# Linear attention beside a routed expert on one core: the layer norm by Ln and Exp on ScalarE, fewer and larger first loads, and a rewritten order of the head

## The chip, the cores and the metric

The kernel runs on one core of a Trainium2 chip. The metric is device time in microseconds (us) of one execution; lower is better. Times shown are the median of several runs, and one further execution was taken with the hardware profiler. TensorE is called PE here, VectorE DVE, ScalarE ACT, GpSimd POOL, and SyncE, which issues most of the DMAs, SP. PEld is PE's weight load, which runs beside its matmuls.

## The reference

```
x = A_x                                   # 1 x 2048 x 640, bf16
xn = layernorm(x)                         # (x - mean) / sqrt(var + 1e-5), no gain, no bias
out = x + A(xn, A_wqkv, A_wo) + B(xn, B_w_r, B_w_gate, B_w_up, B_w_down)

A: q, k, v = xn @ wqkv, 32 heads of 20 columns each
   phi(t) = where(t > 0, t + 1, exp(t)) + 1e-6
   kv = sum over s of phi(k)^T v ;  z = sum over s of phi(k)
   o  = phi(q) kv / (phi(q) z + 1e-6) ;  result o @ wo
B: r = xn @ w_r ;  the 8 rows of largest r go through
   y = (silu(xs @ w_gate) * (xs @ w_up)) @ w_down, times sigmoid(r)
   result: xn, with y added in these 8 rows
```

## The kernel before

The 2048 rows are 16 tiles of 128 rows. Everything is in SBUF: `XX[:, t, 1, :]` is the raw x of tile t, `XX[:, t, 0, :]` its normalised form, `xnT` the transposed normalised rows (5 blocks of 128 columns), `wk` the k part of `wqkv`, `pk` phi(k). The whole kernel is one hand-written order of instructions: the program text is the order in which each engine gets its work, each engine takes its own in that order, and waits are added where data ask for them. An engine whose next instruction waits does nothing else meanwhile.

The head is the part before the loop `for t in range(4, T)`. For tiles 0 to 3 it goes step by step through what the loop does for the others:

- **Norm.** `ln_a(t)` and `ln_b(t)` take statistics of the two halves of 320 columns on DVE, `ln_g(t)` joins them to mean and variance (`MV`). `ln_s(t)` adds epsilon on DVE and takes the square root as a power of 0.5 on POOL. `ln_c(t)` makes mean - x (on DVE in the head, on ACT in the loop), and `ln_xn(t)` takes the reciprocal of the root and multiplies, both on DVE. Tiles 1 and 5 get their statistics from ACT instead (`ln_act`, `ln_msq`, `ln_var`).
- **Transposition.** Tiles 0 to 3 are transposed by PE (`tr_pe`: 3 blocks into one PSUM bank, 2 into the next, each then copied to `xnT` by ACT); the others by a DMA that SP issues (`tr_dma`).
- **K(t)**: xn of tile t times `wk` in two halves of 320 columns, 5 matmuls each. The second half has one column more, which is `w_r`, so that r comes out of the same matmuls; `w_r` is loaded as 5 rows, turned by PE and copied by ACT into that column. The halves of `wk` are two blocks in one tile, of row pitch 320 and 321 elements.
- **PHe, PHr, PHb**: exp and relu of K's halves on ACT, and their combination to `pk` on DVE.
- **G(t)**: the products of xn^T and phi(k), 9 matmuls that add up in PSUM banks 0 to 5 over all tiles. `rcopy1` takes tile 1's r out of bank 5. `ones(t)` sets one column of xn to 1 by POOL before G.

In the loop one tile does K(t), PHb(t-1), `ln_xn(t+2)`, `tr_dma(t+2)`, PHe and PHr, the statistics of tiles t+3 and t+4, and G(t-1).

Behind the loop come q (by blocks of 512 rows), the products with `wv` and `wo` that make `Mb`, the routed rows, and the output; the change touches there only the row pitch of `Mb`, which shares its space with `wk`.

The first loads on SP, in order: x of tiles 0, 1 and 2; the first half of `wk`; x of tile 3; five loads for the second half of `wk` (one for each block of 128 rows); x of tiles 4-5, 6-7, 8-11 and 12-15; and a DMA transposition of zeros into a part of `xnT` that is written again later. While these run, PE multiplies zeros (`warm4`, `warm`), which the kernel sets in SBUF by DVE first. `bm2` is a mask; POOL makes 32 rows of it and three DMAs copy them to the other rows.

Of the kernel before, what the change touches and what calls it, by code (L numbers as in the profile page):

```python
# [38 lines left out]
def kernel(  # L39
# [78 lines left out]
    zero32 = zero[:].bitcast(F32)  # L118

    def warm4(n):  # L120
        for _ in range(n):
            pe.matmul(PS[:, 7, :], lhsT=zero32[:, 0:P],  # L122
                      rhs=zero32[:, 0:256].unsqueeze(1).to_broadcast([P, 2, 256]), start=True, stop=True)

    def warm(n, w=512):
        for _ in range(n):
            pe.matmul(PS[:, 7, 0:w], lhsT=zero[:, 0:P], rhs=zero[:, 0:w], start=True, stop=True)
# [29 lines left out]
    def ln_a(t):  # L157
        sts[t] = tmp.tile([P, 2, nc.vector.BN_STATS_DIM], F32, tag="stats", name="stats", bufs=3)
        dve.bn_stats(out=sts[t][:, 0, :], in_=XX[:, t, 1, 0:320])  # L159
# [787 lines left out]
```

## Time and profile before

| | |
|---|---|
| median of 3 runs | 108.91 us (108.5 to 109.03) |
| the profiled execution | 108.45 us |
| its span, first to last instruction | 106.7 us |
| PE busy | 101.7 us, 95% of the span |
| DVE, ACT, POOL busy | 84.3, 74.8 and 27.8 us |
| loop's first matmul, K(4) | 17.78 us after the span's start |

How to read the rows: in a timeline the first number is the start in us from the span's start, the second the time until the last of the merged instructions ended, then engine, line, operation, output<-inputs, shapes, and xN for N merged instructions; brackets give idle time of the engine before it and what ended it. A queue of DMAs has a q behind its engine (SPq). A wait row has the total, the number of times and the longest wait. A row of a stretch (A:B) has the length, then for PE, PEld, DVE, ACT and POOL the busy time with the number of instructions, then the granted PE clock, the DMA engines' mean busy share and GB/s. A row of a group of instructions has the busy time and the mean ns of one behind the first bar. A row of a DMA has the size of one transfer and the median time from issue to landing in us.

### The profile page before, as it was taken

The numbers are of one execution on the slowest core, as the hardware profiler recorded it, in microseconds if no ns is written. First come the engines' busy times: TensorE is split into PE (matmuls) and PEld (weight loads), VectorE is DVE, ScalarE is ACT, GpSimd is POOL, SyncE is SP. The second block draws the span as 40 slices with busy tenths as digits, with TensorE's granted clock in tenths as the row PEclk, the third lists the DMA queues.
The fourth block names the chain that finished last, engine by engine and source line by source line (L and its number), as shares of the span: only waits on it lengthen the run. The fifth ranks groups of instructions, "written<-read, shape, count | busy, mean of one in ns | idle before, by whom it ended". The sixth has DMA issues, their size and how long they took to land.

```text
span 106.7 us, 2600 instructions
## 1 busy us (share of the span) xinstructions
PE 101.7 (95%) x923; PEld 62.6 (59%) x923; DVE 84.3 (79%) x207; ACT 74.8 (70%) x163; POOL 27.8 (26%) x79
## 2 busy tenths in 40 slices
PE   5979999999999999999999999999999999999990
PEld 1245656666666666667556545655656677777760
DVE  1789997999998999974898996729598696888870
ACT  4649996888877777888497999997688499200000
POOL 7437235456222222000000593500006200000410
PEclk9999999999999999999999999999999999999999
DMA  2999961435566875889998999901560224796344
GB/s 75 272 276 336 339 82 38 81 74 77 112 141 135 118 138 123 175 219 381 234 399 274 352 339 386 311 26 31 170 237 0 63 95 126 177 364 227 123 126 123
DMA packets 23247, 19.68 MB, mean 184 GB/s; under 512 B 10818, under 2 KB 21698, under 8 KB 23234
## 3 DMA queue, kind: packets, MB, share of 16 engines
q1 hardware_dynamic: 22712, 19.45, 65.5%
q8 instruction: 7, 0.11, 0.4%
q0 software_dynamic: 288, 0.01, 0.4%
q10 hardware_dynamic: 234, 0.06, 0.2%
q14 instruction: 6, 0.05, 0.2%
HBM read 13.80 MB, written 3.65 MB: 164 GB/s over the span
## 4 chain that ended last, share of the span: by engine, by line
PE 84%; DVE 7%; POOL 2%; issue 2%; ACT 1%; DVEq 0%; POOLq 0%
PE PS L502 21%; PE PS L755 19%; PE PS L251 15%; PE PS L291 15%; PE PS L296 3%; PE PS L122 2%; PE PS L678 2%; PE PS L715 2%; DVE XX L213 1%; DVE pk L286 1%; POOL s L199 1%; DVE stats L162 1%; PE PS L566 1%; PE PS L737 1%; PE PS L310 1%
## 5 line engine op out<-in xcount | busy, mean ns | idle before, releaser
L251 PE MATMUL PS<-wk,xnT 128*128 128x320 bf16 (+1 forms) x160 | 24.7, 300 | 0.6 <-ACT xnT L224 0.4
L291 PE MATMUL PS<-pk,XX 128*128 128x512 bf16 x80 | 23.2, 378 | 0.1
L502 PE MATMUL PS<-xnT,wq 128*128 128x512 bf16 x100 | 23.0, 380 | 0.0
L755 PE MATMUL PS<-Mb,pqT 128*128 128x320 bf16 (+2 forms) x165 | 22.1, 295 | 0.0
L251 PEld LDWEIGHTS <-xnT 128*128 128x128 bf16 x160 | 15.4, 98 | 7.4 <-ACT xnT L224 0.9
L755 PEld LDWEIGHTS <-pqT 128*128 128x128 bf16 x165 | 15.8, 97 | 6.4 <-issue 0.2
L267 ACT ACTIVATE ek<-PS 128x320 bf16<-128x320 f32 x32 | 14.3, 446 | 5.2 <-PE PS L251 5.2
L502 PEld LDWEIGHTS <-wq 128*128 128x128 bf16 x100 | 11.3, 118 | 9.0
L557 DVE SCALAR_TENSOR_TENSOR pqT<-qe,qr 128x512 bf16<-128x512 bf16 x20 | 13.5, 683 | 2.0 <-ACT qr L509 1.7
L768 DVE TENSOR_TENSOR o<-PS,XX 128x640 bf16<-128x640 f32 x15 | 12.2, 820 | 3.6 <-PE PS L755 2.8
L508 ACT ACTIVATE qe<-PS 128x512 bf16<-128x512 f32 x20 | 12.2, 609 | 3.8 <-PE PS L502 3.3
L270 ACT ACTIVATE rk<-PS 128x320 bf16<-128x320 f32 x32 | 14.4, 449 | 0.0
L199 POOL TENSOR_TENSOR s<-t,halfc 128x1 bf16<-128x1 bf16 x14 | 8.6, 617 | 21.7 <-DVE t L198 21.7
L296 PE MATMUL PS<-pk,XX 128*128 128x128 bf16 x64 | 14.0, 219 | 0.0
L286 DVE SCALAR_TENSOR_TENSOR pk<-ek,rk 128x640 bf16<-128x640 bf16 x16 | 13.0, 815 | 0.9 <-ACT rk L270 0.7
L291 PEld LDWEIGHTS <-XX 128*128 128x128 bf16 x80 | 7.7, 98 | 8.1
L509 ACT ACTIVATE qr<-PS 128x512 bf16<-128x512 f32 x20 | 12.1, 607 | 0.0
L204 ACT ACTIVATE c<-XX,MVf 128x640 bf16<-128x640 bf16 x10 | 8.4, 839 | 1.7 <-DVE MVf L165 1.6
L241 ACT ACTIVATE XX<-XX,MR,SR 128x640 bf16<-128x640 bf16 x11 | 9.4, 914 | 0.0
L159 DVE BATCH_NORM_STATS2 stats<-XX 128x6 f32<-128x320 bf16 x14 | 6.8, 486 | 1.9 <-DMA XX<-in_A_x_dram 1.9
L213 DVE TENSOR_SCALAR XX<-c,SR 128x640 bf16<-128x640 bf16 (+2 forms) x17 | 6.3, 377 | 1.3
L296 PEld LDWEIGHTS <-XX 128*128 128x128 bf16 x64 | 6.2, 97 | 1.3 <-issue 0.4
(125 smaller groups left out, 104.7 us busy)
## 6 DMA issues: line engine op xcount, KB each, us to landing
out_dram<-o SPq DMA_DIRECT2D x15, 160.0 KB, 2.3
wg<-in_B_w_gate_dram SPq DMA_DIRECT2D x5, 384.0 KB, 8.3
wu<-in_B_w_up_dram SPq DMA_DIRECT2D x5, 384.0 KB, 5.9
wd<-in_B_w_down_dram SPq DMA_DIRECT2D x1, 1920.0 KB, 10.7
XX<-in_A_x_dram SPq DMA_DIRECT2D x2, 640.0 KB, 7.1
wv<-in_A_wqkv_dram SPq DMA_DIRECT2D x5, 160.0 KB, 2.9
wq<-in_A_wqkv_dram SPq DMA_DIRECT2D x1, 800.0 KB, 5.4
hi_d<-XX SPq DMA_DIRECT2D x1, 800.0 KB, 4.5
```

The costliest lines, as they stand in the source:

```text
L251: pe.matmul(PS[:, b + h, off(t, h) : off(t, h) + w], lhsT=xnT[:, kc, t * P : (t + 1) * P], rhs=wkh[h][:, kc, 0:w], start=(kc == 0), stop=( ...
L267: act.activation(phis[t][0][:, h * HW : (h + 1) * HW], phi_src(t, h, b), AF.Exp)
L270: act.activation(phis[t][1][:, h * HW : (h + 1) * HW], phi_src(t, h, b), AF.Relu)
L286: dve.scalar_tensor_tensor(out=pk[:, t, :], in0=ek[:], scalar=1.0, in1=rk[:], op0=ALU.min, op1=ALU.add)
L291: pe.matmul(PS[:, a, :], lhsT=lhsT, rhs=pk[:, t, 0:512], start=(t == 0), stop=(t == T - 1),)
L296: pe.matmul(PS[:, 5, a * P : (a + 1) * P], lhsT=lhsT, rhs=pk[:, t, 512:D], start=(t == 0 and a == 0), stop=(t == T - 1), skip_group_check= ...
L502: pe.matmul(PS[:, bank, :], lhsT=by5(wq[:, kc, :])[:, m, :], rhs=xnT[:, kc, tb * TBLK : (tb + 1) * TBLK], start=(kc == 0), stop=(kc == KC ...
L508: act.activation(e, PS[:, bank, :], AF.Exp)
L509: act.activation(r, PS[:, bank, :], AF.Relu)
L557: dve.scalar_tensor_tensor(out=pqT[:, m, tb * TBLK : (tb + 1) * TBLK], in0=e, scalar=1.0, in1=r, op0=ALU.min, op1=ALU.add,)
L755: pe.matmul(PS[:, b_, 0 : c1 - c0], lhsT=pqT[:, kc, t * P : (t + 1) * P], rhs=Mb[:, kc, c0:c1], start=(kc == 0), stop=(kc == KC - 1))
L768: dve.tensor_tensor(out=ot[:].rearrange("p (h c) -> p h c", h=2), in0=PS[:, b : b + 2, 0:HW], in1=XX[:, t, 1, :].rearrange("p (h c) -> p h ...
```

## The change

- The norm becomes one pass: `ln_r(t)` takes Ln of variance + epsilon and then Exp of -0.5 times that, both on ACT with one value a row, which gives 1/sqrt directly; `ln_xn(t)` subtracts the mean and multiplies in one DVE instruction. `ln_s`, `ln_c`, `ln_act` and what belongs to them go, also in the loop. All tiles get their statistics from DVE.
- `wk` has one row pitch of 656 elements: 640 columns, the column of `w_r` at 640, and 15 unused. It comes in two loads of whole rows, 3 blocks and 2.
- Loads on SP, in order: x of tiles 0 and 1, `wk` in two, x of tiles 2-3, 4-7 and 8-11, the transposition of zeros. x of tiles 12-15 is loaded after the transposition of tile 5.
- Tile 3 is transposed by DMA. PE's transposition of tiles 0 to 2 is split in blocks 0-1 and 2-4 (`tr_mm`), with the copies (`tr_cp`) on ACT, or on DVE for the second part of tiles 0 and 2. K of tiles 0 to 2 is split alike: `KA` are its first two matmuls of a half, `KB` the other three.
- The matmuls of zeros take a constant that is there from the program's start, three of them in fp32.
- `bm2`'s rows are copied by POOL, at the start.
- The order of the head is written anew.

```
-    wk = st([P, KC * (D + 1)], BF16, "wk", "wkM")
+    wk = st([P, KC, WS], BF16, "wk", "wkM")
...
-    halfc = st([P, 1], BF16, "halfc")
-    epsb = st([P, 1], BF16, "epsb")
+    eps5 = st([P, 1], F32, "eps5")
+    lnv = st([P, T], F32, "lnv")
-    wkh = [wk[:, 0 : KC * HW].rearrange("p (k c) -> p k c", k=KC),
-           wk[:, KC * HW : KC * (D + 1)].rearrange("p (k c) -> p k c", k=KC)]
...
-    ld(sp, XX[:, 2, 1, :], x_v[:, 2, :])
-    ld(sp, wkh[0], wqkv_v[:, :, D : D + HW])
-    ld(sp, XX[:, 3, 1, :], x_v[:, 3, :])
...
+    for a, b in ((0, 3), (3, KC)):
+        ld(sp, wk[:, a:b, 0:D], wqkv_v[:, a:b, D : 2 * D])
+    for a, b in ((2, 4), (4, 8), (8, 12)):
+        ld(sp, XX[:, a:b, 1, :], x_v[:, a:b, :])
+    sp.dma_start_transpose(xnT[:, 0:4, S - P : S], zero[:])
+
+    def warm4(w):
+        pe.matmul(PS[:, 7, 0:w], lhsT=nc.const_aps.tensor(0.0, (P, P), F32),
+                  rhs=nc.const_aps.tensor(0.0, (P, w), F32), start=True, stop=True)
+
...
-    warm4(1)
+    warm4(512)
+    warm4(256)
     pe.transpose(PS[:, 3, :].bitcast(BF16)[:, 0:KC], wr[:], ident[0:KC, 0:KC])
-    warm4(1)
-    warm(1)
-    act.copy(wkh[1][:, :, HW], PS[:, 3, :].bitcast(BF16)[:, 0:KC])
-    for kc in range(KC):
-        ld(sp, wkh[1][:, kc, 0:HW], wqkv_v[:, kc, D + HW : 2 * D])
+    warm4(512)
+    act.copy(wk[:, :, D], PS[:, 3, :].bitcast(BF16)[:, 0:KC])
...
+    def ln_r(t):
+        act.activation(lnv[:, t : t + 1], MV[:, t, 1:2], AF.Ln, bias=eps5[:])
+        act.activation(SR[:, t : t + 1], lnv[:, t : t + 1], AF.Exp, scale=-0.5)
+
+    def ln_xn(t, parts=((0, D),)):
+        for a, b in parts:
+            dve.tensor_scalar(out=XX[:, t, 0, a:b], in0=XX[:, t, 1, a:b], scalar1=MVf[:, t, 0:1],
+                              scalar2=SR[:, t : t + 1], op0=ALU.subtract, op1=ALU.mult)
+
+    TRP = ((0, 2), (2, KC))
+
+    def tr_mm(t, h, b0):
+        k0, k1 = TRP[h]
+        pt = PS[:, b0 + h, :].bitcast(BF16)
+        for kc in range(k0, k1):
+            pe.transpose(pt[:, (kc - k0) * P : (kc - k0 + 1) * P], XX[:, t, 0, kc * P : (kc + 1) * P], ident[:])
+
+    def tr_cp(t, h, b0, eng):
+        k0, k1 = TRP[h]
+        src = PS[:, b0 + h, :].bitcast(BF16)[:, 0 : (k1 - k0) * P].rearrange("p (k c) -> p k c", c=P)
+        dst = xnT[:, k0:k1, t * P : (t + 1) * P]
         if eng is act:
...
+            act.copy(dst, src)
         else:
...
+            dve.tensor_copy(dst, src)
 
...
-    def K(t, hs=(0, 1), b=6):
+    def K(t, hs=(0, 1), b=6, ks=range(KC)):
...
-                    rhs=wkh[h][:, kc, 0:w],
+                    rhs=wk[:, kc, h * HW : h * HW + w],
...
+    def bm2_copies(gs):
         for g in gs:
+            pool.tensor_copy(bm2[32 * g : 32 * g + 32, :], bm2[0:E2, :])
...
```

The new order of the head, from behind the definitions to the loop:

```
consts_e(); bm2_copies((1, 2, 3)); KA, KB = (range(0, 2), range(2, KC)); ln_a(0); ln_b(0); ln_a(1)
ln_g(0); ln_b(1); ln_r(0); ln_g(1); ln_xn(0, ((0, 2 * P),)); ln_r(1); ln_xn(0, ((2 * P, D),))
tr_mm(0, 0, 0); ln_xn(1); tr_cp(0, 0, 0, act); tr_mm(0, 1, 0); ones(0); tr_mm(1, 0, 2)
tr_cp(0, 1, 0, dve); K(0, (0,), 6, KA); tr_cp(1, 0, 2, act); tr_mm(1, 1, 2); ones(1)
K(0, (0,), 6, KB); ln_a(2); tr_cp(1, 1, 2, act); K(0, (1,), 6, KA); ln_b(2); PHe(0, 0)
K(1, (0,), 4, KA); PHr(0, 0); ln_g(2); K(0, (1,), 6, KB); ln_a(3); ln_r(2); K(1, (1,), 4, KA); ln_b(3)
K(1, (0,), 4, KB); PHe(0, 1); ln_xn(2); PHr(0, 1); ln_g(3); tr_mm(2, 0, 0); PHe(1, 0, 4); PHb(0)
K(1, (1,), 4, KB); tr_cp(2, 0, 0, act); tr_mm(2, 1, 0); ones(2); ln_r(3); K(2, (0, 1), 6, KA)
tr_cp(2, 1, 0, dve); PHr(1, 0, 4); ln_a(4); PHe(1, 1, 4); ln_xn(3); tr_dma(3); ones(3); PHr(1, 1, 4)
K(2, (0, 1), 6, KB); rcopy1(5); ln_b(4); PHe(2, 0); G(0, (0, 1, 4, 2, 3)); PHb(1); PHr(2, 0)
PHe(2, 1); ln_g(4); ln_a(5); ln_r(4); ln_b(5); PHr(2, 1); G(1); ln_xn(4); tr_dma(4); ln_g(5); PHb(2)
ln_r(5); K(3); ln_xn(5); tr_dma(5); ld(sp, XX[:, 12:16, 1, :], x_v[:, 12:16, :]); ln_a(6); PHa(3)
ln_b(6); G(2); ln_g(6); ln_r(6)
```

The loop:

```
     for t in range(4, T):
         K(t)
         ones(t)
         PHb(t - 1)
-        if t + 3 < T and t < 5 and t + 3 not in ACTS:
+        if t + 3 < T and t < 5:
             ln_a(t + 3)
         if t + 2 < T:
             ln_xn(t + 2)
             tr_dma(t + 2)
         PHa(t)
         if t + 3 < T:
-            if t + 3 in ACTS:
-                ln_act2(t + 3)
-                ln_var(t + 3)
-            else:
-                ln_b(t + 3)
-                ln_g(t + 3)
-                ln_s(t + 3)
-            ln_c(t + 3, act)
-        if t + 4 < T and t + 4 in ACTS:
-            ln_act1(t + 4)
-        if t + 4 < T and t >= 5 - 1 and t + 4 not in ACTS:
+            ln_b(t + 3)
+            ln_g(t + 3)
+            ln_r(t + 3)
+        if t + 4 < T and t >= 5 - 1:
             ln_a(t + 4)
...
```

More of the change, by code (lines that the diff above doesn't have):

```diff
@@ L26 @@
 ZD = 4 * P
-ACTS = ()
 TF = 11
+WS = 656
 BF16 = mybir.dt.bfloat16
@@ L390 @@
-    ln_var(1)
+    ln_b(1)
+    ln_r(0)
+    ln_g(1)
+    ln_xn(0, ((0, 2 * P),))
+    ln_r(1)
+    ln_xn(0, ((2 * P, D),))
+    tr_mm(0, 0, 0)
+    ln_xn(1)
+    tr_cp(0, 0, 0, act)
+    tr_mm(0, 1, 0)
+    ones(0)
+    tr_mm(1, 0, 2)
+    tr_cp(0, 1, 0, dve)
+    K(0, (0,), 6, KA)
+    tr_cp(1, 0, 2, act)
+    tr_mm(1, 1, 2)
+    ones(1)
+    K(0, (0,), 6, KB)
     ln_a(2)
-    ln_xn(1)
+    tr_cp(1, 1, 2, act)
+    K(0, (1,), 6, KA)
     ln_b(2)
+    PHe(0, 0)
+    K(1, (0,), 4, KA)
+    PHr(0, 0)
```

182 lines of the change are left out of this document (54 added, 128 removed).

## The prediction

> **What bounds the kernel now.** I read the page first (who is busy), then the waits of PE, then the timelines of PE, DVE, ACT and SP over the first 18 us.
>
> ```profile
> span 106.7 us, 2600 instructions
> PE 101.7 (95%) x923; PEld 62.6 (59%) x923; DVE 84.3 (79%) x207; ACT 74.8 (70%) x163; POOL 27.8 (26%) x79
> PE PS L122 <- DVE MVf L109: 1.2, 1, 1.2
> PE PS L251 <- ACT xnT L224: 0.4, 1, 0.4
> PE PS L220 <- DVE XX L213: 0.2, 1, 0.2
> ```
>
> PE is busy for 95% of the span, and the three waits are all that it has, all at the start. The change leaves the matmuls as they are, except five PE transposes. So its effect is how much earlier or later PE gets past the head. As the mark I take the start of K(4), the first projection of the main loop; behind it PE is a closed row. The timeline of PE up to there:
>
> ```profile
> 5.22 0.38 PE L127 MATMUL PS<-zero 128*128 128x512 bf16 x1
> 5.82 0.48 PE L220 MATMUL PS<-ident,XX 128*128 128x128 bf16 x5 [0.22 <-DVE XX L213]
> 6.73 0.85 PE L251 MATMUL PS<-wk,xnT 128*128 128x320 bf16 x5 [0.43 <-ACT xnT L224]
> 7.70 1.83 PE L251 MATMUL PS<-wk,xnT 128*128 128x321 bf16 x10
> 9.54 0.45 PE L220 MATMUL PS<-ident,XX 128*128 128x128 bf16 x5
> 9.83 2.23 PE L251 MATMUL PS<-wk,xnT 128*128 128x321 bf16 x15
> 11.90 0.45 PE L220 MATMUL PS<-ident,XX 128*128 128x128 bf16 x5
> 12.19 0.38 PE L291 MATMUL PS<-pk,XX 128*128 128x512 bf16 x1
> 13.49 1.53 PE L251 MATMUL PS<-wk,xnT 128*128 128x320 bf16 x10
> 15.18 0.38 PE L291 MATMUL PS<-pk,XX 128*128 128x512 bf16 x1
> 17.78 1.53 PE L251 MATMUL PS<-wk,xnT 128*128 128x320 bf16 x10
> 19.15 0.38 PE L291 MATMUL PS<-pk,XX 128*128 128x512 bf16 x1
> ```
>
> K(4) starts at 17.78, and its 10 matmuls take 19.15 - 17.78 = 1.37 us (0.137 each). G(0) takes 13.49 - 12.19 = 1.30, five transposes 12.19 - 11.90 = 0.29. From the first K at 6.73 the work is 4 K (5.48), 3 G (3.90) and the transposes of tiles 1 to 3 (0.87): 10.25 of the 11.05 us. The missing 0.8 shows: the x10 at 7.70 lasts until 9.54, 0.47 over 1.37; K(3) at 13.49 is through at 14.86, and the next row starts at 15.18, 0.32 later. The change can thus gain 0.8 from these holes, 0.29 from tile 3's transposes, and whatever the first K starts before 6.73.
>
> **The change, part by part.** First the chain of tile 0. DVE and ACT now, and the forms nearest to the new ones:
>
> ```profile
> 3.15 0.50 DVE L159 BATCH_NORM_STATS2 stats<-XX 128x6 f32<-128x320 bf16 x1 [1.92 <-DMA XX<-in_A_x_dram]
> 3.56 0.48 DVE L162 BATCH_NORM_STATS2 stats<-XX 128x6 f32<-128x320 bf16 x1
> 4.07 0.21 DVE L165 BATCH_NORM_AGGREGATE MVf<-stats 128x2 bf16<-128x12 f32 x1
> 4.31 0.16 DVE L198 TENSOR_SCALAR t<-MVf 128x1 bf16<-128x1 bf16 x1
> 5.24 0.16 DVE L211 RECIPROCAL SR<-s 128x1 f32<-128x1 bf16 x1 [0.16 <-POOL s L199]
> 5.44 0.51 DVE L213 TENSOR_SCALAR XX<-c,SR 128x384 bf16<-128x384 bf16 x2
> 5.87 0.48 DVE L159 BATCH_NORM_STATS2 stats<-XX 128x6 f32<-128x320 bf16 x1
> 9.10 0.39 DVE L213 TENSOR_SCALAR XX<-c,SR 128x640 bf16<-128x640 bf16 x1
> 10.53 0.81 DVE L286 SCALAR_TENSOR_TENSOR pk<-ek,rk 128x640 bf16<-128x640 bf16 x1
> L631 ACT ACTIVATE gl<-ge 1x8 f32<-1x8 f32 x1 | 0.2, 208 | 0.0
> L224 ACT COPY xnT<-PS 128x256 bf16<-128x256 bf16 x4 | 1.5, 386 | 0.0
> ```
>
> The statistics go out every 0.41 (3.15 to 3.56); an aggregate behind its own statistics comes 0.51 later, and its successor 0.24 after it. New order on DVE: ln_a(0) 3.15, ln_b(0) 3.56, ln_a(1) 3.97, ln_g(0) 4.38, ln_b(1) 4.62, ln_g(1) 5.13. The square root with reciprocal leaves DVE and POOL (4.31 to 5.40 now, hidden by nothing) for ln_r, two [128,1] activations on ACT. No row has that form; L631 is the nearest, 0.21 each, so 0.45 with the hand-overs: 4.64 to 5.1, under ln_b(1) and ln_g(1). The first part of ln_xn(0), 256 columns, then starts at 5.37 (now 5.44, 384 columns). Transposes at 5.7, copy of 256 columns 0.39 instead of 384, first K at 6.45 instead of 6.73: 0.28 earlier. The new warm-up is three fp32 matmuls that wait for no memset; by the present ones (ended 5.2 from a start at 1.23, with 0.3 for the bf16 one) it is over by 5.5, under that chain.
>
> Next the loads, the weightiest edit. SP's timeline, DMA by stretch (last column GB/s), and issue to landing of the first and the fourth x load, of the weight's first half and of the transposes:
>
> ```profile
> 0.79 1.35 SPq L104 DMA_DIRECT2D XX<-in_A_x_dram  x3
> 2.18 0.43 SPq L104 DMA_DIRECT2D wk<-in_A_wqkv_dram  x1
> 2.66 0.52 SPq L104 DMA_DIRECT2D XX<-in_A_x_dram  x1
> 2.00:3.50 1.50, 1.50 (x4) 0.25 (x2) 0.35 (x1) 0.11 (x2) 1.12 (x4) 1.00 0.95 272
> 3.50:4.50 1.00, 1.00 (x2) 0.48 (x3) 0.93 (x5) 0.97 (x4) 0.00 (x0) 1.00 0.83 203
> 4.50:7.00 2.50, 1.85 (x10) 0.51 (x9) 1.88 (x8) 1.64 (x5) 1.83 (x5) 1.00 1.12 331
> XX<-in_A_x_dram SPq DMA_DIRECT2D x1, 160.0 KB, 2.3
> XX<-in_A_x_dram SPq DMA_DIRECT2D x1, 160.0 KB, 4.0
> xnT<-zero SPq DMA_TRANSPOSE x1, 7.6
> xnT<-XX SPq DMA_TRANSPOSE x8, 2.6
> ```
>
> Now x of tile 2 is the third load and DVE uses it at 5.87 without a wait. After the change x of tiles 2 and 3 is one load behind x0, x1 and all of wk: 320 + 800 + 320 = 1440 KB, 1475 kB, must pass. By the rows 408 kB have moved at 3.5. Fed at 331 GB/s from there, the rest takes 3.2 us: moved at 6.7. A load lands later than that sum, because the 16 engines don't end together: the fourth x load (1040 KB with all ahead of it, 1065 kB) is through by the same rows at 4.5 + (1065 - 408 - 203)/331 = 5.9 and lands at 2.66 + 4.0 = 6.66, 0.8 later; the first (164 kB, through at 2.6) lands at 3.1, 0.5 later. Bounds for tile 2: early, the full rate from 3.5 on and the lag of 0.5, 7.2; late, the 203 GB/s of 3.5 to 4.5 come again: 4.5 + 864/331 + 0.8 = 7.9. I take 7.4, nearer to the early end: seven loads of long rows are queued by about 4.1 (0.47 an issue), so nothing small stands between them; but the low rate may be no matter of queueing. "DMA: Bandwidth & Descriptors" of the Trainium skill (Specifications) gives about 358 GB/s as the HBM limit of one core; an estimate by that page, 1067 kB from 3.5 with the lag of 0.8, is 7.3, and the trace's stretches lie below that limit.
>
> From this landing, called L, on which all of DVE now waits at ln_a(2), DVE goes on in order: ln_a(2) L+0.03, ln_b(2) +0.41, ln_g(2) +0.52, ln_a(3) +0.24, ln_b(3) +0.41, ln_xn(2) +0.41, its 0.39 and a hand-over of 0.06: transposes of tile 2 on PE at L + 2.47 (ln_r(2), 0.5 after the aggregate, lies under the statistics of tile 3). With L = 7.4 that is 9.87. PE has by then K(0) and all of K(1) but 0.41: from 6.45 2.3 us and the transposes 0.17, so it stands from 8.93, **a new hole of 0.9 us**. From the transposes to K(4) there remain 0.29 + 0.41 + K(2) 1.37 + G(0) 1.30 + G(1) 1.30 + K(3) 1.37 + G(2) 1.30 = 7.34 us, and two small waits: PE's K(2) for ACT's copy, 0.07 (0.28 transposes + 0.39 copy + 0.1 against 0.69 of cover), G(0) for ACT's last reader of bank 5, 0.09. K(4) = L + 9.96 = **17.36, 0.42 before now**. ACT waits too: ln_r(2) stands ahead of the exponentials of K(0)'s second half and of K(1) and of tile 2's copy. It is released at L + 1.2 = 8.6, and two activations of 0.2 and three of 0.33 (an estimate from the copy row, less its overlap) later the copy is free at 10.0, needed at 10.15: hidden, with 0.15 to spare. Were L no bound (6.6 or less, DVE free), it would be 16.66, 1.12 before now; each 0.1 us of L costs 0.1.
>
> Tile 3 by DMA: its ln_xn ends near L + 4.5 = 11.9, landing 2.6 later at 14.5; PE asks for K(3) at L + 7.28 = 14.7. Hidden by G(0) and G(1), with 0.2 to spare. It is behind one thing on SP's queue, the transposes of zeros.
>
> Without effect on the mark: the norm in one pass takes the subtraction off ACT, the reciprocal off DVE and the power off POOL, but in the loop all three have slack under PE (shares above; cover: 2.67 us of K and G a tile); bm2's copies go from SP to an idle POOL; x 12 to 15 is loaded later, its first reader comes in the loop. The padded rows of wk:
>
> ```profile
> L251 PE MATMUL PS<-wk,xnT 128*128 128x321 bf16 x80 | 13.9, 301 | 0.1
> L251 PE MATMUL PS<-wk,xnT 128*128 128x320 bf16 x80 | 13.5, 299 | 0.4 <-ACT xnT L224 0.4
> ```
>
> The second half, now in rows of an odd 321 elements, is 2 ns slower a matmul, of which a column is 0.4: 80 x 1.6 = 0.13 us if the pitch is the cause, else nothing; I take 0.13.
>
> **Sum.** -0.42 - 0.13 = -0.55 us. The profiled run took 108.45 us (span 106.7 and 1.75 around it) and would take 107.9. It lies 0.46 below the median of the runs shown (108.91; 108.5 to 109.03), so for a median: 108.91 - 0.55 = **108.35**. A measurement of this kernel can tell about 0.5%, 0.54 us: the forecast stands on that edge.
>
> **The rivals.** *Tile 2 early.* The larger packets end the low rate and the lag, and L is 7.0 or less: -0.95 to -1.25, 107.7 to 108.0. For it: the first load's lag of 0.5; against: 0.8 as soon as loads are queued. *Tile 2 late.* L from 7.7 to 8.3: -0.25 to +0.35, 108.7 to 109.3, no change that could be told. For it: the 203 row. *The column of w_r waits for the weights (slower).* act.copy into column D of wk stands first on ACT, ahead of ln_r(0). If the program makes it wait for the two loads around that column, it runs at their landing (1147 kB: 4.5 + 536/331 + 0.8 = 6.9), and all of ACT behind it: first K at about 8.5 instead of 6.45, ln_a(2) at 8.7, K(4) at 18.6: +0.7 net, 109.6. It decides as soon as the copy is later than 4.4. Against: 16 elements of padding separate column and next row. *Tile 3's transposition late.* The zeros, issued at 7.85, landed after 7.6 us, behind all loads then queued; after the change 1280 KB of x stand before them, through at 7.1 + 3.9 = 11 and landed up to 12.5. If the zeros land past 13.3, half of tile 3's 2.6 behind them is past 14.7, and K(3) waits: up to 1 us, 108.4 to 109.4. The same page (HWDGE ordering) has descriptors consumed in ring order on each engine, and the 7.6 us agree.
>
> **How the numbers follow.** L from 7.0 to 7.7, the forecast: 0.47. Early: 0.15. Late: 0.17. Column: 0.11. Tile 3: 0.10. Of the forecast's cases (-0.95 to -0.25) six in ten are over 0.5%: faster 0.29 + 0.15 = 0.44; no change 0.18 of it, 0.12 of the late case and 0.02 of tile 3: 0.32; slower the rest, 0.24. The forecast's own range is 107.9 to 108.7. The range given, 107.5 to 109.6, takes in the early case nearly whole, the late one, and the column's lower half.
>
> **What would show it.** Right: the first K on PE at 6.4 to 6.5; DVE's first wait after 3.15 at line ln_a(2), until 7.4; a hole on PE of 0.9 before tile 2's transposes at 9.9; K(4) near 17.3; after that no wait of PE. Wrong: no such wait of DVE (then K(4) at 16.7), ACT's copy of the column behind 4.4, a wait of K(3) for a DMA, or a PE in the loop that waits for ACT.

## The result and the profile after

The changed kernel takes 110.25 us (median of 4 runs, 109.78 to 110.41) against 108.70 for the one before (4 runs, 108.41 to 109.03): a ratio of 1.0135 with a 95% interval of [1.0087, 1.0182]. It is slower by a little over 1%; forecast were 108.35 and a range of 107.5 to 109.6. Here and below, executions that took over 1.5% more than the fastest of their kernel are left out, and each ratio is to executions of the kernel before that were taken beside it. The profiled execution took 110.36 us, 1.91 more than before's 108.45. Its page, first lines and one line of the DMA queues:

```profile
span 108.6 us, 2525 instructions
PE 101.3 (93%) x909; PEld 63.1 (58%) x919; DVE 81.2 (75%) x180; ACT 69.7 (64%) x171; POOL 16.6 (15%) x58
q8 instruction: 7, 0.11, 0.4%
```

The other engines got lighter as the change means them to: DVE 84.3 to 81.2, ACT 74.8 to 69.7, POOL 27.8 to 16.6. PE does the same work in a longer span. Its waits, all of them:

```profile
PE PS L205 <- DMA xnT<-XX: 1.4, 1, 1.4
PE PS L171 <- DVE XX L162: 1.0, 1, 1.0
PE PS L118 <- PEq L884: 0.8, 1, 0.8
PE PS L205 <- DMA wk<-in_A_wqkv_dram: 0.3, 1, 0.3
```

The last three lie in the head. The first, one wait of 1.4 us for a transposition by DMA, is in no case of the prediction at this place. PE's timeline says where, and DVE's what comes ahead of it:

```profile
6.85 0.43 PE L205 MATMUL PS<-wk,xnT 128*128 128x320 bf16 x2 [0.35 <-DMA wk<-in_A_wqkv_dram]
10.82 0.28 PE L171 MATMUL PS<-ident,XX 128*128 128x128 bf16 x2 [1.05 <-DVE XX L162]
15.57 1.53 PE L205 MATMUL PS<-wk,xnT 128*128 128x320 bf16 x10
16.93 0.38 PE L245 MATMUL PS<-pk,XX 128*128 128x512 bf16 x1
19.82 1.54 PE L205 MATMUL PS<-wk,xnT 128*128 128x320 bf16 x10 [1.42 <-DMA xnT<-XX]
8.54 0.49 DVE L148 BATCH_NORM_STATS2 stats<-XX 128x6 f32<-128x320 bf16 x1 [1.99 <-DMA XX<-in_A_x_dram]
```

K(4) starts at 19.82 instead of 17.78. G(2) starts at 16.93 and takes 1.30 as before, so PE asks for K(4) at 18.23: the wait costs 1.59 (1.42 in the brackets, because ends of matmuls are modelled). Without it K(4) would be 0.45 later than before, not 0.42 earlier: L, the landing that DVE waits for, came at 8.52 instead of 7.4. From K(4) to the end there is 110.36 - 19.82 = 90.54, before 90.67: behind the mark nothing changed (0.13 less). So 1.91 = 1.59 (tile 4's transposition late) + 0.45 (the head, by L) - 0.13.

Why the transposition of tile 4 was late. SP issues the three of tiles 3 to 5 at 12.86, 15.20 and 16.50:

```profile
12.86 4.86 SPq L183 DMA_TRANSPOSE xnT<-XX  x3
16.90:17.75 0.85, 0.85 (x9) 0.46 (x6) 0.44 (x2) 0.85 (x3) 0.00 (x0) 1.00 0.45 93
17.75:18.70 0.95, 0.65 (x5) 0.20 (x3) 0.77 (x2) 0.53 (x3) 0.00 (x0) 1.00 2.00 130
18.70:19.80 1.10, 0.00 (x0) 0.00 (x0) 1.10 (x4) 0.00 (x0) 0.00 (x0) 1.00 0.30 42
```

Tile 3's landed at 15.43, 2.57 after its issue. Of tile 4's 16 completions (one by each DMA engine) 15 came between 17.62 and 17.81, 2.6 after the issue; the last came at 19.78. In between, at 17.75, the trace's packet records hold one packet of 16,384 bytes that took 0.93 us, on the queue that the page calls "q8 instruction". There are 7 such packets in a run (the q8 line: 0.11 MB); PE and PEld have 909 + 919 instructions, one packet for 261 on average, and the experiments below move it by adding PE instructions: it is PE's code.

A transposition has 640 packets of 256 bytes, which take 18 ns (median), and 32 of 4 bytes that report its end, two for each completion. Tile 4's data had all started by 17.28, and 30 of its 32 reports by 17.30. The last two started at 18.66, as the code packet ended (18.68). So one engine's report waited for the code. Why it was not already out at 17.30, before the code packet's own record begins, the records do not show. Tile 5's data, from 17.69 on, are slowed too: 18 of their packets, started from 18.0 to 18.5, took 1,004 to 1,296 ns. In the row 17.75:18.70 the share of time in packets goes from 0.45 to 2.00, mostly for that reason, while 130 GB/s move.

In the kernel before the same packet came too: at 17.02, 1.32 us long. Tile 4's transposition had just landed (17.02), and tile 5's, issued at 17.75 before the packet's end, landed 2.58 later as usual. It cost nothing. That is the theory, called F: **what decides is whether PE's code packet, whose time depends on the number of PE instructions ahead of it, falls into a transposition that PE is about to need.** The rivals: X, the load of x 12 to 15 that now stands behind tile 5's transposition (issued 17.77, when the stall is on); S, two transpositions in flight at once; and L alone, the late loads, which can account for 0.45 of the 1.91.

### The profile page after: what moved, and what is told of

The parts are those of the page before. It is cut to its first block, busy times and chain, and to the rows that moved or that the text cites. A ratio compares the mean times of both kernels' runs of the same rounds, so it can differ in the third digit from the quotient of the medians.

```text
span 108.6 us, 2525 instructions
## 1 busy us (share of the span) xinstructions
PE 101.3 (93%) x909; PEld 63.1 (58%) x919; DVE 81.2 (75%) x180; ACT 69.7 (64%) x171; POOL 16.6 (15%) x58
## 2 busy tenths in 40 slices
DMA packets 23039, 19.82 MB, mean 182 GB/s; under 512 B 11250, under 2 KB 21490, under 8 KB 23026
## 4 chain that ended last, share of the span: by engine, by line
PE 77%; DMA 10%; DVE 5%; issue 2%; SPq 2%; ACT 1%; DVEq 0%
PE PS L455 20%; PE PS L708 19%; PE PS L205 15%; PE PS L245 12%; DMA XX<-in_A_x_dram 5%; DMA xnT<-XX 4%; PE PS L250 3%; SPq L102 2%; PE PS L631 2%; PE PS L668 1%; DVE pk L240 1%; DVE stats L151 1%; PE PS L519 1%; DVE stats L148 1%; PE PS L690 1%
## 5 line engine op out<-in xcount | busy, mean ns | idle before, releaser
L245 PE MATMUL PS<-pk,XX 128*128 128x512 bf16 x75 | 22.4, 379 | 0.0
L224 ACT ACTIVATE rk<-PS 128x320 bf16<-128x320 f32 x32 | 13.8, 432 | 0.0
L245 PEld LDWEIGHTS <-XX 128*128 128x128 bf16 x80 | 7.8, 98 | 8.2
L148 DVE BATCH_NORM_STATS2 stats<-XX 128x6 f32<-128x320 bf16 x16 | 7.3, 458 | 3.9 <-DMA XX<-in_A_x_dram 3.9
L151 DVE BATCH_NORM_STATS2 stats<-XX 128x6 f32<-128x320 bf16 x16 | 7.7, 479 | 0.0
L256 POOL MEMSET XX<- 128x1 bf16 x16 | 1.6, 103 | 39.2 <-DMA xnT<-XX 18.6
L162 DVE TENSOR_SCALAR XX<-XX,MVf,SR 128x640 bf16<-128x640 bf16 (+2 forms) x17 | 7.2, 429 | 0.0
L545 DVE TENSOR_TENSOR pqT<-pqT,R 128x1280 bf16<-128x1280 bf16 x8 | 6.5, 817 | 0.6 <-DMA R<-rd_d 0.6
```

The costliest lines, as they stand in the source:

```text
L224: act.activation(phis[t][1][:, h * HW : (h + 1) * HW], phi_src(t, h, b), AF.Relu)
L245: pe.matmul(PS[:, a, :], lhsT=lhsT, rhs=pk[:, t, 0:512], start=(t == 0), stop=(t == T - 1),)
```

## The experiments

### Moving the code packet, in the changed kernel and in the one before

Three kernels differ from their parent only in the warm-up, whose matmuls multiply zeros; each bf16 matmul is two PE instructions (a weight load and the matmul), and more of them move the code packet earlier.

```
changed kernel, with 34 and with 26:
-    warm4(512)
+    for _ in range(34):
+        pe.matmul(PS[:, 7, 0:P], lhsT=zero[:, 0:P], rhs=zero[:, 0:P], start=True, stop=True)
     act.copy(wk[:, :, D], ...)
kernel before:
-    warm(1)
+    for _ in range(8):
+        warm(1, 64)
```

> The changed kernel with the last fp32 matmul of zeros (1.8 us) replaced by 34 bf16 ones of 128 columns (1.9 us): 64 more instructions on PE ahead of the head, the same time. Theory F (the 16 KB instruction packet of PE, at 17.75 in the changed kernel, sits on one DMA engine while tiles 4 and 5 are being transposed by DMA, and holds tile 4 back by 2 us): the packet comes near 13.1, between the zeros and tile 3, tile 4 lands 2.6 after its issue, K(4) starts near 18.2 instead of 19.8, and the kernel is 1.4 to 1.6 us faster than the changed one, about 108.8. Rival X (the load of x 12 to 15 holds tile 4's transposition back) and rival S (two transposes issued 1.3 us apart do): K(4) stays near 19.8 and the time near 110.2.

> As the one with 34, but with 26: the packet should come near 14.3, while tile 3 is being transposed. Theory F: tile 3 lands 1 to 2 us late (16.5 to 17.5 instead of 15.4), K(3) waits for it (16.5 to 17.5 instead of 15.57), tile 4 is not held back and K(4) starts between 18.8 and 19.8. Rivals X and S: K(3) at 15.6 and K(4) at 19.8, as in the changed kernel.

> The kernel before with its one bf16 matmul of 512 zeros replaced by eight of 64: 14 more instructions on PE, about the same time. Theory F: PE's 16 KB packet comes near 15.9 instead of 17.02, while tile 4 is being transposed (15.5 to 16.6), tile 4 lands near 18.5 to 19 instead of 16.95, K(4) starts at 18.6 to 19.1 instead of 17.78, and the kernel before becomes 0.8 to 1.3 us slower with no other change. Rivals X and S: no change, K(4) at 17.8.

Measured: 34 matmuls 110.50 us, ratio to the kernel before 1.0151 [1.0105, 1.0196]; 26 matmuls 108.94, 1.0018 [0.9996, 1.0039]; the kernel before with 14 more PE instructions 109.71, 1.0092 [1.0064, 1.0121]. PE's rows, in this order (the third and fourth of 26 matmuls, the last of the kernel before):

```profile
16.45 1.54 PE L206 MATMUL PS<-wk,xnT 128*128 128x320 bf16 x10 [1.26 <-DMA xnT<-XX]
19.12 1.53 PE L206 MATMUL PS<-wk,xnT 128*128 128x320 bf16 x10
14.92 1.53 PE L206 MATMUL PS<-wk,xnT 128*128 128x320 bf16 x10
17.78 1.54 PE L206 MATMUL PS<-wk,xnT 128*128 128x320 bf16 x10
19.07 1.55 PE L252 MATMUL PS<-wk,xnT 128*128 128x320 bf16 x10 [0.92 <-DMA xnT<-XX]
```

With 34 the wait moves from K(4) to K(3), with 26 neither waits, and the kernel before, which had no such wait, gets one at its K(4) and is 1 us slower by nothing but 14 PE instructions. (The version with 34 has its K(4) at 19.12, 0.7 ahead of the changed kernel, and is no faster: in its profile PE waits 0.90 for DVE at 95.00, in the output. I did not follow that up.) The two expectations for the changed kernel were the wrong way round: I had the packet meeting nothing with 34 and tile 3 with 26. The packet came 0.2 to 0.4 later than expected, and I had the time of tile 3's data wrong: they move from about 1.2 behind the issue for 0.9 us. The packet records beside the issues and landings (the last completion) of eight kernels, in us:

| kernel | code packet, start + duration | tile 3: issue, landing | tile 4: issue, landing | who waited |
|---|---|---|---|---|
| before | 17.02 + 1.32 | by PE | 14.42, 17.0 | none |
| before, 14 instructions more | 16.79 + 1.15 | by PE | 14.63, 19.0 | K(4) 0.9 |
| changed | 17.75 + 0.93 | 12.86, 15.43 | 15.20, 19.78 | K(4) 1.4 |
| changed, 26 | 14.54 + 1.57 | 12.21, 14.78 | 14.55, 17.73 | none of the two |
| changed, 34 | 13.46 + 1.29 | 12.31, 16.41 | 14.65, 17.26 | K(3) 1.3 |
| changed, x 12-15 later | 16.86 + 0.93 | 11.96, 14.52 | 14.30, 18.89 | K(4) 1.4 |
| the same, 24 | 14.93 + 1.38 | 12.65, 15.21 | 14.99, 17.94 | none |
| the same, 46 | 12.75 + 0.94 | 12.76, 15.31 | 15.10, 17.72 | none |

Where tile 3 or tile 4 meets no packet, it lands 2.5 to 2.6 after its issue. A packet at the issue (within 0.1 of it) costs nothing to 0.6. One that comes 1.1 to 2.57 behind the issue costs 1.5 to 2 in the four late rows, and in three kernels further below. But the time behind the issue does not decide alone: tile 3 of the versions with 26 and 24 met a packet 2.33 and 2.28 behind its issue and lost nothing, and the kernel before, 2.60 behind, neither. The packet records show three cases. In the versions with 26 and 24 all 32 reports of tile 3 had started 0.2 before the code packet. In the changed kernel, with x 12-15 later, in the kernel before with 14 more, and in two kernels below, 30 were out and the last two started within 0.02 of the code packet's end. With 34 the packet came with the first data (13.46 and 13.47), and all 16 completions are late; so it is in the third kernel below, with 19 matmuls. What separates the first case from the second, I cannot say in advance: the records do not tell which engine carries the code.

Rival S falls: in the kernel before with 14 instructions more tile 5 is issued at 17.96, when the packet is over and 15 of tile 4's 16 completions are in (17.43), and tile 4 is late all the same; the version with 46 has tiles 4 and 5 in flight together (issued at 15.10 and 16.39), and tile 4 lands after 2.62.

### Taking the load of x 12 to 15 out of the way

```
     sp: tr_dma(5)
-    ld(sp, XX[:, 12:16, 1, :], x_v[:, 12:16, :])
...
             tr_dma(t + 2)
+        if t == 5:
+            ld(sp, XX[:, 12:16, 1, :], x_v[:, 12:16, :])
```

> The changed kernel with the load of x 12 to 15 moved from behind tile 5's transposition to behind tile 7's. Rival X: tile 4 lands 2.6 after its issue, K(4) near 18.2, 1.5 us faster. Theory F and rival S: tile 4's last engine still lands near 19.8, K(4) and the time as in the changed kernel.

Measured 109.91 us (2 runs), ratio 1.0112 [1.0043, 1.018]; the profiled one 109.45. The last row is of the version with 26 matmuls, which has the load in its old place.

```profile
9.92 0.28 PE L171 MATMUL PS<-ident,XX 128*128 128x128 bf16 x2 [0.97 <-DVE XX L162]
14.67 1.53 PE L205 MATMUL PS<-wk,xnT 128*128 128x320 bf16 x10
18.93 1.54 PE L205 MATMUL PS<-wk,xnT 128*128 128x320 bf16 x10 [1.44 <-DMA xnT<-XX]
23.85 1.54 PE L206 MATMUL PS<-wk,xnT 128*128 128x320 bf16 x10 [0.56 <-DMA xnT<-XX]
```

The wait for tile 4 stays as it was, with nothing loaded beside it: for tile 4, rival X falls. For the tile behind the load it holds. In the version with 26 the load is issued at 17.92, tile 6's transposition at 18.89, and this lands 4.91 later: the last row is K(6), which waits for it, and that is most of what this version lost behind its K(4) (109.07 - 17.78 = 91.29 to the end, 90.67 in the kernel before). Moved behind tile 7, the load does the same to tile 8, 4.3 to 5.0 us from issue to landing in all eight versions that have it there, where the kernel before has 2.56; most of it is hidden there.

This profile is also the prediction's head nearly to the number, though by two errors that cancel, L 0.2 too early and the way from L to K(4) 0.25 too long: L is 7.61, tile 2's transposes at 9.92 (forecast 9.87), the hole ahead of them 0.97 (0.9), K(3) at 14.67 (14.7). PE asks for K(4) at 16.03 + 1.30 = 17.33, behind G(2) (forecast 17.36), and gets it at 18.93.

### Small matmuls at no cost of PE's time

The 26 matmuls above were longer than the one they replace (2.4 against 1.8 us), so that the first K came at 6.95. Here they stand where PE waits for `w_r` anyway, and have 32 columns. The other version has 22 of them, and 24 of 64 columns in place of the last `warm4(512)`. In both the load of x 12 to 15 is moved as above.

```
     warm4(512)
-    warm4(256)
+    for _ in range(24):
+        pe.matmul(PS[:, 7, 0:32], lhsT=zero[:, 0:P], rhs=zero[:, 0:32], start=True, stop=True)
```

> The changed kernel with x of tiles 12 to 15 behind tr_dma(7), and with the second fp32 warm-up matmul (256 columns) replaced by 24 bf16 ones of 32 columns: some 45 PE instructions more ahead of the first transposes, at no time of PE's. Theory F: the code packet moves from 16.9 to about 14.2, between the landing of tile 3's transposition (14.5) and the data of tile 4's (from about 15.5): K(3) and K(4) wait for no DMA or by under 0.3, K(4) at 17.4 to 17.7, 108.0 to 108.4, the prediction's number. If the packet still touches the end of tile 3's transposition, K(3) waits up to 1 us and the time is 108.8 to 109.3. If F is false, as the kernel with the late load alone: K(4) near 18.9, 109.9.

> As the kernel with 24 small matmuls, but 22 of 32 columns in place of the second fp32 warm-up matmul and 24 of 64 columns in place of the third: some 88 PE instructions more. Theory F: the code packet moves to about 11.9, while only x of tiles 8 to 11 is under way and before tile 3's transposition has data (from about 13): no wait of PE for a DMA at K(3) or K(4), K(4) at 17.3 to 17.6, 107.9 to 108.3. If the packet comes at 13 instead, K(3) waits 1.3 as with 34 matmuls and the time is 109.5 or more. If F is false, 109.9.

Measured: 24 matmuls 108.64 us (9 runs, 107.72 to 108.97), ratio 0.9983 [0.9954, 1.0013]; 46 matmuls 109.43 (7 runs, 108.57 to 109.88), 1.0050 [1.0015, 1.0085]. PE with 24 (three rows) and with 46 (four):

```profile
10.62 0.29 PE L172 MATMUL PS<-ident,XX 128*128 128x128 bf16 x2 [1.06 <-DVE XX L163]
15.36 1.53 PE L206 MATMUL PS<-wk,xnT 128*128 128x320 bf16 x10
18.03 1.53 PE L206 MATMUL PS<-wk,xnT 128*128 128x320 bf16 x10
6.66 0.69 PE L207 MATMUL PS<-wk,xnT 128*128 128x320 bf16 x2
7.46 3.20 PE L207 MATMUL PS<-wk,xnT 128*128 128x320 bf16 x15
10.72 0.28 PE L173 MATMUL PS<-ident,XX 128*128 128x128 bf16 x2
18.13 1.53 PE L207 MATMUL PS<-wk,xnT 128*128 128x320 bf16 x10
```

In both the wait of K(4) is gone, though the packet came 0.7 and 0.85 later than expected (14.93 and 12.75); at 24 matmuls that is worth 1.3 us of median against the same kernel without them. The forecast times, 108.0 to 108.4 and 107.9 to 108.3, were missed all the same, and the rows say by what: L is 8.31 and 8.41 here, so K(4) is at 18.03 and 18.13, not 17.4. That is the second loss, which the packet does not explain. With 46 the first K matmuls also ran slower: 0.69 for two and 3.20 for fifteen, where the changed kernel has 0.43 and 2.49; the small matmuls had ended at 4.98, half a microsecond ahead of the transposes, and the granted clock is 1.00 in these stretches; the cause is not shown. The hole ahead of tile 2 took up most of it here. Why the median of the version with 46 lies 0.74 above its profiled run of 108.69 is open.

### The head without the wait for x of tiles 2 and 3

```
     ld(sp, XX[:, 1, 1, :], x_v[:, 1, :])
-    for a, b in ((0, 3), (3, KC)):
+    ld(sp, XX[:, 2, 1, :], x_v[:, 2, :])
+    for a, b in ((0, 2), (2, KC)):
         ld(sp, wk[:, a:b, 0:D], ...)
-    for a, b in ((2, 4), (4, 8), (8, 12)):
+    for a, b in ((3, 4), (4, 8), (8, 12)):
```

> The changed kernel with x of tiles 12 to 15 behind tr_dma(7), and with x of tile 2 loaded by itself ahead of the weights, which come as 2 blocks and 3. The prediction's step L (all of DVE waits at ln_a(2) for x of tiles 2 and 3 behind the weights): that wait goes, and PE's first K waits for the weights instead; the hole ahead of tile 2's transposes falls from 0.9-1.1 to below 0.5, tile 2's transposes at 9.3 to 9.8, what K(4) could start at falls to 17.0-17.3. Theory F: the code packet still comes in the last third of tile 4's transposition (16.5 to 17), so K(4) waits for it at 18.4 to 18.9 all the same: 109.2 to 109.8. If L were what made the changed kernel slow, 108.3 or less.

The load of x 12 to 15 is moved here too. Measured 110.01 us, ratio 1.0105 [1.0038, 1.0173]. DVE, then PE:

```profile
8.34 0.50 DVE L149 BATCH_NORM_STATS2 stats<-XX 128x6 f32<-128x320 bf16 x1 [0.75 <-DMA XX<-in_A_x_dram]
9.75 0.45 DVE L163 TENSOR_SCALAR XX<-XX,MVf,SR 128x640 bf16<-128x640 bf16 x1 [0.52 <-ACT SR L159]
7.93 2.20 PE L206 MATMUL PS<-wk,xnT 128*128 128x320 bf16 x15 [0.78 <-DMA wk<-in_A_wqkv_dram]
10.25 0.28 PE L172 MATMUL PS<-ident,XX 128*128 128x128 bf16 x2
19.27 1.54 PE L206 MATMUL PS<-wk,xnT 128*128 128x320 bf16 x10 [1.44 <-DMA xnT<-XX]
```

DVE no longer waits for tile 2, whose statistics run from 6.47. But behind them, in its order, stand the statistics of tile 3, and DVE now waits for those rows (until 8.34) with tile 2's normalisation queued behind. PE's hole has moved to the weights, whose second load lands at 7.89 (7.67 in the changed kernel). The time of tile 2's transposes, 10.25, was missed by half a microsecond, and PE asks for K(4) at 16.36 + 1.30 = 17.66, later than the 17.33 with x 12 to 15 moved alone. The code packet at 17.20, 2.57 behind the issue of tile 4's transposition, costs 1.6 as before (1.44 in the brackets). So the head has two limits close together, the loads and DVE's order; to take away one shows the other.

### The norm in one pass, alone in the kernel before

The main lines; besides, the second half of tile 1's statistics on ACT moves behind tile 0's Ln and Exp.

```
-        pool.tensor_tensor(out=ss[t][:], in0=t2[:], in1=halfc[:], op=ALU.pow)
+        act.activation(lnv[:, t : t + 1], MV[:, t, 1:2], AF.Ln, bias=eps5[:])
+        act.activation(SR[:, t : t + 1], lnv[:, t : t + 1], AF.Exp, scale=-0.5)
     def ln_xn(t, parts=((0, D),)):
...
+            dve.tensor_scalar(out=XX[:, t, 0, a:b], in0=XX[:, t, 1, a:b], scalar1=MVf[:, t, 0:1],
+                              scalar2=SR[:, t : t + 1], op0=ALU.subtract, op1=ALU.mult)
```

> The kernel before with the one-pass norm alone: Ln and Exp on ACT in place of the power on POOL, the reciprocal and the subtraction on DVE or ACT; tiles 1 and 5 keep their statistics on ACT, loads, transposes and the order of everything else stay. The prediction's view: what it saves in the chain of tile 0 (first K up to 0.3 earlier) is lost again, because the second half of K(0) waits for the weights and the loop is bound by PE: K(4) within 0.3 of 17.78, time 108.3 to 108.9 against 108.6. Theory F (PE's code packet beside tile 4's transposition decides): the same number of PE instructions, so the packet stays near 17.0; tile 4's transposition is issued no later than now (14.4) and is through before it: no wait of PE for a DMA. Rival N (the norm on ACT is itself what costs): PE waits for ACT in the loop, over 109.2.

Measured 110.67 us, ratio 1.018 [1.014, 1.0219]: slower by 2 us, where I expected nothing. Three of PE's waits and one of DVE's; Ln of tile 3 on ACT; and K(4):

```profile
PE PS L207 <- DVE XX L200: 1.0, 1, 1.0
PE PS L238 <- ACT xnT L211: 0.8, 1, 0.8
PE PS L238 <- DMA wk<-in_A_wqkv_dram: 0.7, 1, 0.7
DVE XX L200 <- ACT SR L193: 5.3, 6, 1.6
12.53 0.40 ACT L192 ACTIVATE lnv<-MVf,eps 128x1 f32<-128x1 bf16 x1
19.87 1.53 PE L238 MATMUL PS<-wk,xnT 128*128 128x320 bf16 x10
```

PE waits for no transposition by DMA; the packet (18.57) meets none. K(4) comes 2.09 later than before, so the whole cost lies in the head, and not in the loop where rival N had it. The rows put it down to ACT's order. Power and reciprocal were on POOL and DVE, past all that ACT had queued. Put on ACT at the places of the old steps, Ln and Exp stand behind the copies and exponentials of the tiles before: tile 3's mean and variance are there at 9.88, its Ln starts at 12.53. DVE waits six times for them, 5.3 us in all. The two instructions are cheap (0.29 and 0.20); the queue they stand in is not. And what they gain for tile 0 is lost at once, since the first K then waits for the weights (6.72, and 6.73 before). So the norm in one pass needs another order of the head. What it gains in the order that the change brings along no run tells: that order was not run with the old norm.

### A version meant to beat both

With the loads as above, PE can do the first two blocks of K(0) and K(1), in both halves, before it needs the second weight load; DVE normalises tile 2 before it turns to tile 3, and tile 3 before tile 4:

```
+ K(0,(0,),6,KA); ...; K(0,(1,),6,KA); ln_a(2); ...; ln_b(2); K(1,(0,1),4,KA); ln_g(2); ln_r(2)
+ K(0,(0,),6,KB); ln_xn(2); PHe(0,0); PHr(0,0); K(0,(1,),6,KB); ln_a(3); PHe(0,1)
+ K(1,(0,),4,KB); ln_b(3); tr_mm(2,0,0); PHr(0,1); tr_cp(2,0,0,dve); ln_g(3)
+ K(1,(1,),4,KB); PHe(1,0,4); tr_mm(2,1,0); ones(2); tr_cp(2,1,0,dve); ln_r(3)
+ K(2,(0,1),6,KA); PHb(0); ...; ln_xn(3); tr_dma(3); ...; K(2,(0,1),6,KB); rcopy1(5); ln_a(4); ln_b(4)
```

The lines replace the order of the head between the first matmuls of K(0) and the exponentials of K(2). It ran with 19 small matmuls in the warm-up and with none (`warm4(256)` kept).

> A version meant to beat both kernels. The changed kernel with x of tile 2 loaded ahead of the weights (2 blocks and 3), x of tiles 12 to 15 behind tr_dma(7), 19 bf16 matmuls of 32 columns in place of the second fp32 warm-up matmul, and the head reordered: the first two blocks of K(0) and K(1) in both halves before anything that needs the second weight load, ln_xn(2) ahead of ln_a(3) on DVE, tile 2's copies on DVE, ln_xn(3) ahead of ln_a(4). Theory (L and F): PE has 1.1 us of work ahead of the second weight load (landing 7.9), tile 2's transposes come at 9.2 instead of 10.2-10.8, K(3) at 14.0 to 14.3, K(4) at 16.6 to 17.2; the code packet comes about 0.2 before K(3), behind tile 3's landing and ahead of tile 4's data: 107.3 to 107.9. If the packet meets the end of tile 3's or tile 4's transposition, K(3) or K(4) waits 0.8 to 1.5 for it and the time is 108.3 to 109.2. If DVE, not the loads, sets the head, K(4) stays at 17.7 to 18.

> The same reordered head without the 19 small matmuls, so with the code packet some 36 PE instructions, about 2.3 us, later than in its twin: near 16. Theory F: tile 4's transposition is then under way (issued about 13.9, landing 16.5 undisturbed); if the packet comes while it has data, K(4) waits up to 1.5: 108.4 to 109.2, 0.8 to 1.5 above the twin. If it comes behind tile 4's landing, the two are equal within 0.3. If F is false, equal.

Measured: 19 matmuls 109.32 us, ratio 1.0032 [0.9988, 1.0077]; none 109.77, 1.0083 [1.0036, 1.0129]. PE with 19, then with none:

```profile
9.29 0.28 PE L173 MATMUL PS<-ident,XX 128*128 128x128 bf16 x2
14.50 1.52 PE L207 MATMUL PS<-wk,xnT 128*128 128x320 bf16 x10
18.71 1.54 PE L207 MATMUL PS<-wk,xnT 128*128 128x320 bf16 x10 [1.38 <-DMA xnT<-XX]
8.86 0.28 PE L172 MATMUL PS<-ident,XX 128*128 128x128 bf16 x2
14.07 1.53 PE L206 MATMUL PS<-wk,xnT 128*128 128x320 bf16 x10
18.23 1.54 PE L206 MATMUL PS<-wk,xnT 128*128 128x320 bf16 x10 [1.33 <-DMA xnT<-XX]
```

The new order does its part: tile 2's transposes come at 9.29 and 8.86 instead of 10.82, without a hole, and K(3) at 14.50 and 14.07 instead of 15.57. With none, K(4) came at 18.23 after a wait of 1.3. Neither reached its time (both lie above even the range for a packet that meets the transposition), because the packet came at 15.49 and 16.10, 1.1 and 2.1 behind the issue of tile 4's transposition, which landed 4.27 and 4.22 after it. Nineteen matmuls had moved it by 0.6, where I had reckoned with 2.3. So one more step, 25 and 28 matmuls in place of 19:

```
-    for _ in range(19):
+    for _ in range(25):
```

> The reordered head with 25 small matmuls of zeros in place of 19: 12 more PE instructions ahead of the first transposes, nothing else. With 19 the packet came at 15.49, 1.1 behind the issue of tile 4's transposition (14.39), and K(4) waited 1.4 for it. Theory F: it now comes at 14.4 to 14.9, within 0.4 of that issue and behind tile 3's landing, and touches neither: no wait of K(4) for a DMA, K(4) at 16.8 to 17.3, 107.4 to 107.9. If it still comes past 15, K(4) waits and the time is 109 as with 19. If F is false, 109.3.

> The same with 28: 18 PE instructions more than with 19, packet at 13.9 to 14.4. Theory F: if it starts no more than 0.3 ahead of tile 3's landing (14.2), as with 26 matmuls in the changed kernel, neither K(3) nor K(4) waits: 107.4 to 107.9. If it starts earlier, K(3) waits up to 1 us: 108.2 to 108.8. If F is false, 109.3.

Measured: 25 matmuls 108.13 us (12 runs, 107.77 to 108.81), ratio 0.9951 [0.9922, 0.998]; 28 matmuls 108.38 (107.59 to 109.08), 0.997 [0.9939, 1.0001]. PE with 25, K(3), K(4) and K(8):

```profile
14.65 1.53 PE L207 MATMUL PS<-wk,xnT 128*128 128x320 bf16 x10
17.31 1.53 PE L207 MATMUL PS<-wk,xnT 128*128 128x320 bf16 x10
28.30 1.54 PE L207 MATMUL PS<-wk,xnT 128*128 128x320 bf16 x10 [0.16 <-DMA xnT<-XX]
```

The packet came at 14.47 with 25 and at 14.27 with 28, where it was meant to; tile 4's transposition was issued at 14.54 and landed at 17.18 (2.64), and K(4) no longer waits. Twelve PE instructions of zeros are worth 1.2 us of median (0.8% by the ratios). The version with 25 is faster than the kernel before by 0.5%, with an interval that leaves 1 out; its median lies 2.1 us below that of the changed kernel. With 28 the interval takes in 1. They stayed 0.2 and 0.5 above the time expected. With 25, K(4) at 17.31 is 0.47 ahead of the kernel before; K(8) then waits 0.16 for tile 8's transposition, which stands behind the load of x 12 to 15 (4.70 from issue to landing); PE's last matmul ended at 103.50 against 103.85; and the span is 106.7 in both, because the last output took 0.35 more, which I did not follow up.

## Why the prediction was wrong, by its own steps

**The step that failed** is the way from tile 2's transposes to K(4). "From the transposes to K(4) there remain" 7.34 us of PE's work "and two small waits": that has K(4) start right behind G(2) and puts the wait for tile 4's transposition at nothing, without a reason. Measured, the last completion came at 19.78 and K(4) waited 1.59. The prediction charged tile 3's transposition (issued, landing 2.6 later, asked for 0.2 after that) and not tile 4's, whose slack is hardly larger: without the packet it would have landed at 17.81, and PE asks at 18.23, 0.42 later (tile 3: 0.14). Neither had a rival by which a transposition by DMA could take longer than the 2.6 of its row, except behind the zeros. The row is a median of eight in the kernel before, and there the first code packet fell between tile 4's and tile 5's. What the prediction says of the time behind the mark, "PE is a closed row", did hold (90.54 and 90.67). The code's seven packets stand on the page in one line, 0.4% of the DMA engines' time; a share says nothing of who is held up. The sum with this term is 1.4 to 1.6 us higher. That the packet causes it is shown, in both kernels, by moving it, and by the last reports that start as it ends; what inside the DMA engines holds them is not.

Of this the Trainium skill has the first half: "Runtime: NRT & Kernel Launch" (Instruction fetch mechanics) says that each engine's code is brought in by a DMA queue of its own in blocks of 16 KiB, 256 instructions, and that the cost of a block's boundary is "mostly hidden". The size and the number agree with the trace (16,384 bytes; 7 packets for 1,828 instructions). For PE's own stream the cost is hidden here as well: no wait of PE names it. For a transposition beside it, it is not where the two meet as above: 1.5 to 2 us.

**L was mis-sized**, which is the other 0.45. Forecast 7.4, bounds 7.2 to 7.9; measured 8.52, and in the five other profiles with this order of loads 7.97, 7.87, 7.61, 8.31 and 8.41. Two stretches of the changed kernel:

```profile
3.00:4.00 1.00, 1.00 (x4) 0.34 (x4) 0.87 (x3) 0.10 (x1) 0.86 (x4) 1.00 0.80 146
4.50:7.00 2.50, 2.08 (x11) 0.56 (x10) 1.98 (x7) 1.74 (x6) 0.73 (x3) 1.00 1.05 355
```

The low rate that I hoped might go with larger packets came, earlier and lower: 146 GB/s from 3.0 to 4.0 (223 in the kernel before), then 234 from 3.5 to 4.5 (203). So the small packets of the kernel before were not its cause alone; the rate after it is a little higher (355, 331). By the packet records 1475 kB had moved at 7.04, where the sum has 6.7: the rate cost 0.3. The rest, 0.8, is lag: 14 of the 16 engines had ended x of tiles 2 and 3 between 6.81 and 7.55, two at 8.41 and 8.52, and two were late by a microsecond in both weight loads before (6.72 and 6.81; 7.54 and 7.67). I had allowed 0.5 to 0.8, and it was 1.5. The two laggards set L, and whatever made them late varies from run to run; I did not find it. The rival "tile 2 late" had the effect, with an end at 8.3 that was 0.2 too early, but for another reason, the low rate.

**What was right.** The relation K(4) = L + 9.96 holds without the packet: L + 9.71 in the profiled run, 9.72 with 24 and 46 matmuls and with x 12 to 15 later; it is 0.25 too long, and each 0.1 of L does cost 0.1. (With 26 it is 9.91; there the first K came late.) The hole ahead of tile 2 was 1.05 (0.9 forecast), DVE's wait stands at ln_a(2), K(3) came 7.05 behind L (7.28), and tile 3 landed 0.14 ahead of it (0.2). The chain of tile 0 is as worked out, 6.50 without PE's wait of 0.35 for the weights, which I did not have (the first K came at 6.85, forecast 6.45); it costs nothing, for the hole follows. Ln and Exp:

```profile
4.55 0.29 ACT L157 ACTIVATE lnv<-MVf,eps 128x1 f32<-128x1 bf16 x1 [0.48 <-DVE MVf L154]
4.88 0.20 ACT L158 ACTIVATE SR<-lnv 128x1 f32<-128x1 f32 x1
3.90 0.18 ACT L132 COPY wk<-PS 128x5 bf16<-128x5 bf16 x1 [1.81 <-PE PS L130]
L205 PE MATMUL PS<-wk,xnT 128*128 128x321 bf16 x80 | 13.9, 300 | 0.0
```

together 0.53 with their hand-over, 0.45 forecast. ACT's copy of the column runs at 3.90 and waits for no load: the rival of the column did not happen. Nor did the zeros delay tile 3: they landed at 12.93, ahead of its data. The pitch of wk's rows gained 1 ns a matmul in the odd form (301 to 300), not 2. That the norm has no effect on the mark was argued from shares of busy time; in the old order it costs 2 us. No run takes the pitch, the warm-up in fp32 or bm2's copies alone.

## What to carry to other kernels

An average of transfers with slack to spare hides what they cost when something large stands in their way: before you charge a DMA its usual time on a path with a few tenths of a microsecond of slack, look in the trace for large packets of other queues, the code of the busiest engine among them, for large loads issued just ahead of it, and at the time from issue to the last of the 16 completions. A rival that falls for one transfer can hold for the next: the load of x 12 to 15 did nothing to tile 4, and held up tile 6, or tile 8 where it was moved. When an edit of a few instructions moves a kernel by 1%, and a neighbouring edit moves it back, ask first whether the edit only shifted something that follows the instruction count; adding a few instructions that do nothing is a cheap test, and here the tuning itself. And a cheap instruction moved to another engine costs what stands ahead of it in that engine's order.
